# The second attention product as four 64x64 matmuls per tile, and a new order of work in a fused attention and routed-MLP kernel

## The chip, the core and the metric

The kernel runs on one core of a Trainium2 chip. The metric is the device time of one execution in microseconds. Each engine (TensorE, VectorE, ScalarE, GpSimd, and SyncE, which only starts transfers) has its own list of instructions and takes them in the order in which they were written; an instruction that waits holds up all that is behind it on its engine.

## The reference

Two stages follow each other. The first is an attention without scores between positions: for each of 8 batches and 8 heads, with 576 positions of 64 numbers,

```
q_s = softmax(q, over the 64 numbers)      # exp, divided by its sum
k_s = softmax(k, over the 576 positions)
kv  = k_s^T v                              # 64x64 for each head
x   = q_s kv                               # 576x64, heads side by side: 576x512
```

The second picks, in each batch, the 128 positions with the largest `x . w_gate`, and adds `sigmoid(score) * relu(xe w1) w2` to these rows alone (w1 is 512x1024, w2 1024x512). All data are float32.

## The kernel before, in words

A unit is a batch and four of its heads: 16 units, two to a batch. Positions lie on partitions so that a unit's q, k and v are tiles of 128 partitions, 4 heads, R = 5 rows, 64 numbers. Three buffers for each of q, k, v hold the units to come. A main loop has 20 slots `s`. In slot s the kernel ends unit s and begins unit s+1, and from slot 4 on it also does half of a batch's MLP: `mlp1` in even slots, `mlp2` in odd ones, each in 8 pieces that the program strews between the attention's steps. The names of the steps:

- `k_exp`, `q_exp`: the exponentials, on ScalarE. `v_copy`: copies v beside a column of ones, on VectorE.
- `kv_mm` (line 233): 20 matmuls with 128 rows and 64 columns of weights; two of them fill the width of the array. `kv_out` takes the sums out of PSUM and makes the operand of the next product, with one more column for the gate score.
- `q_t`, `q_t_last` (lines 260, 269): the transposes of exp(q); ScalarE (line 262) and VectorE (line 271) copy them to SBUF as `qT`, scaled by 1/sum of k.
- `x_mm(s, i)` (line 280): the second product for two heads, i = 0 and 1. Before, the two heads' 64x64 kv stand on the diagonal of a 128x128 operand `kv_diag` whose other half is zero, and 5 full matmuls of 132 columns do it.
- `x_out` (lines 292 to 298): VectorE divides by the sum of exp(q), writes `xs`, and keeps the score column. `x_store` sends `xs` to memory from SyncE's queue, behind which the loads of unit s+4 stand.
- `score`, `score_row`, `compare`, `pick`, `gate`: once per batch, the ranks of the scores. `score_row` (line 331) turns the scores by TensorE, five `compare` (line 344) count ranks on VectorE, `pick` (lines 364, 368) finds the rows by a VectorE operation `hit` and five small matmuls, and gathers them.
- `turn` (line 397), `mlp1` (411), `mlp2` (421), `finish` (429): the MLP of a picked batch.

Each float32 matmul stands in the trace as two records with their own weight loads: 5 matmuls of `x_mm` are 10 records, 20 of `kv_mm` are 40. The order inside the loop is written out by hand (`tc.manual_schedule`); before, the setup ahead of it is ordered by a scheduler.

Of the kernel before, what the change touches and what calls it, by code (L numbers as in the profile page):

```python
# [17 lines left out]
def kernel(  # L18
# [20 lines left out]
    nc = tc.nc  # L39
# [12 lines left out]
    G = 12  # L52
# [5 lines left out]
    WARM = 12  # L58
# [30 lines left out]
    def load(u, which, queues=(nc.sync, nc.sync)):  # L89
        b, qd = units[u]  # L90
        for what in which:
# [3 lines left out]
            for n, rows in enumerate((R, N2)):  # L95
                queues[n].dma_start(  # L96
                    out=t[n::2, :, :rows].rearrange("p h r d -> p h (r d)"),
                    in_=bass.AP(tensor=src.tensor, offset=first + n * R * D,
                                ap=[[9 * D, 64], [SD, 4], [1, rows * D]]))

    for n in range(LD):
        for what in "kvq":
            (nc.vector if n == 0 else nc.gpsimd).memset(raw[what][n][:, :, N2], 0.0)
    load(0, "k", (nc.sync, nc.scalar))
    load(0, "vq")
# [7 lines left out]
    warm = const.tile([P, 1], F32, name="warm")  # L113
    nc.scalar.activation(out=warm, in_=ones_b[:, :1], func=AF.Exp)
    ones_f = const.tile([P, P + 4], F32, name="ones_f")
    nc.vector.memset(ones_f, 1.0)
    w_ps = bank("tp", 2)
    w_ps2 = bank("tp", 2)
    for n in range(24):
        a, c = ((0, 0), (1, 1), (0, 1), (1, 0))[n % 4 if n >= 12 else n % 2]  # L120
        nc.tensor.matmul(out=(w_ps, w_ps2)[a][part(c), :66], lhsT=ones_f[part(a), :64],
                         rhs=ones_f[part(a), :66], start=True, stop=True)
    for n in range(WARM):
        nc.tensor.matmul(out=w_ps[:, :P], lhsT=ones_b[:, :P], rhs=ones_b[:, :P], start=True, stop=True)

    wg = const.tile([P, NQ, 2, D], F32, name="wg")
    for h in range(2):
        nc.scalar.dma_start(out=wg[part(h)].rearrange("p a i d -> p (a i) d"),
                            in_=bass.AP(tensor=moe_w_gate.tensor, offset=moe_w_gate.offset + h * D,
                                        ap=[[0, 64], [2 * D, 2 * NQ], [1, D]]))  # L130
    w1 = const.tile([P, KD, F], F32, name="w1")
# [4 lines left out]

    side = const.tile([P, 2], F32, name="side")
    nc.vector.memset(side, 0.0)
# [8 lines left out]
    v_ones, kv_diag = [], []  # L147
    for n in range(2):
# [4 lines left out]
        t = const.tile([P, 2, 2, C], F32, name=f"kv_diag{n}")  # L153
        nc.vector.memset(t, 0.0)
        kv_diag.append(t)
    for h in range(2):
        nc.vector.memset(side[part(h), h:h + 1], 1.0)
    qrec = const.tile([P, NU, 2, G], F32, name="qrec")
    krec = const.tile([P, NU, 2], F32, name="krec")


    x_buf = []
    for n in range(2):
        t = ps.tile([P, 2, 512], F32, tag=f"x{n}", name=f"x{n}", bufs=1)
        nc.vector.memset(t[:, 1, 4 * C:6 * C], 1.0)
        x_buf.append(t)
# [22 lines left out]
    def late_constants():  # L189

        nc.vector.tensor_single_scalar(odd_p, odd_p, 1, op=OP.bitwise_and)
        nc.vector.tensor_tensor(out=whole, in0=whole, in1=odd_p.to_broadcast([P, B * R]), op=OP.add)
        nc.vector.tensor_single_scalar(whole, whole, 1, op=OP.arith_shift_right)
        nc.vector.tensor_single_scalar(rest, whole, 31, op=OP.bitwise_and)
        nc.vector.tensor_tensor(out=whole, in0=whole, in1=rest, op=OP.subtract)
        nc.vector.tensor_copy(out=vals[:, :, :, 0], in_=whole.rearrange("p (b r) -> p b r", b=B))
        nc.vector.tensor_copy(out=vals[:, :, :, 1], in_=rest.rearrange("p (b r) -> p b r", b=B))
        nc.vector.memset(valid_r[:, 0], 1.0)
        nc.vector.memset(valid_r[:, 1], 0.0)
        nc.vector.memset(valid_r[:, 2], UP)  # L200
        nc.vector.tensor_copy(out=valid_r[:, 0, N2:], in_=valid)
        nc.vector.tensor_copy(out=valid_r[:, 1, N2:], in_=beyond)
        nc.vector.tensor_scalar(valid_r[:, 2, N2:], valid, UP, None, op0=OP.mult)
        for r in range(R):
# [324 lines left out]
    with tc.manual_schedule():  # L529
# [11 lines left out]
        for s in range(NU + LAG):  # L541
# [19 lines left out]
            if s == NU:  # L561
                chosen = B - 1
# [92 lines left out]
```

## Time and profile before

| | us |
|---|---|
| median of 3 runs (276.93 to 279.32) | 279.23 |
| the profiled execution | 278.86 |
| its span in the trace | 277.0 |
| TensorE matmul busy | 226.2 (82%) |
| VectorE busy | 131.1 (47%) |
| ScalarE busy | 92.0 (33%) |
| GpSimd busy | 27.8 (10%) |

Busy time is a sum over the whole span; the span has a start (to 14.7 us), four slots without MLP work (to 68.9), twelve with it (to 229), and an end in which only the last batches' MLP is left. A slot begins here with the first transpose of `q_t`. The granted clock of TensorE has two levels, shown as 1.00 (2.4 GHz) and 0.50 (1.2 GHz); a stretch that holds both shows a value between.

### The profile page before, as it was taken

The page shows a single profiled execution, that of the slowest core. Times are in us where ns is not written, and L with a number is a line of the kernel's source. Part 1 is how long each engine was busy: PE and PEld are TensorE (multiplying, and loading weights), DVE is VectorE, ACT ScalarE, POOL GpSimd, SP SyncE. Part 2 cuts the span into 40 slices and gives each one's busy share as a digit, 9 for nine tenths or more (in the row PEclk, how much of TensorE's full clock was granted, in tenths as well). Part 3 has the DMA queues.
Part 4 walks back from the last instruction along what each step waited for, and adds up shares of the span by engine and source line. Part 5 has one row for each costly group of instructions (what it writes and reads, how often), then busy time and mean ns, then how long its engine had stood idle before and what let it go on. Part 6 is the DMA issues. An engine that isn't in the chain of part 4 may idle for free.

```text
span 277.0 us, 4988 instructions
## 1 busy us (share of the span) xinstructions
PE 226.2 (82%) x1933; PEld 181.1 (65%) x1933; DVE 131.1 (47%) x435; ACT 92.0 (33%) x162; POOL 27.8 (10%) x74
## 2 busy tenths in 40 slices
PE   5367656566998999899989998999889998598990
PEld 4356646455895679567956795679567974584940
DVE  3275433943375347634764476447644656521001
ACT  2254422603434343434343434343435321110000
POOL 4000010011001110111011101110111011200001
PEclk9999775757899999999999999999999999799997
DMA  5999999296919292929292919291302032010101
GB/s 166 351 346 322 317 359 315 91 297 213 278 34 300 98 286 73 305 93 283 75 311 85 296 65 290 107 289 69 116 28 102 3 119 93 38 38 2 40 7 41
DMA packets 39328, 46.68 MB, mean 169 GB/s; under 512 B 2944, under 2 KB 36736, under 8 KB 39296
## 3 DMA queue, kind: packets, MB, share of 16 engines
q1 hardware_dynamic: 37200, 41.69, 47.2%
q0 software_dynamic: 1280, 4.20, 4.2%
q10 hardware_dynamic: 816, 0.39, 0.6%
q8 instruction: 17, 0.28, 0.4%
q14 instruction: 15, 0.12, 0.1%
HBM read 34.73 MB, written 11.53 MB: 167 GB/s over the span
## 4 chain that ended last, share of the span: by engine, by line
PE 56%; DVE 21%; DMA 9%; issue 5%; ACT 4%; SPq 3%; POOL 0%; POOLq 0%; ACTq 0%; DVEq 0%
PE mm L411 14%; PE mm L421 12%; PE x L280 12%; PE tp L233 9%; DMA v<-in_v_dram 7%; DVE xs L295 6%; PE tp L260 5%; DVE junk L344 4%; DVE v_ones L223 4%; SPq L96 2%; DMA q<-in_q_dram 2%; DVE qrec L292 2%; PE tp L331 2%; ACT qT L262 2%; SPq L303 1%
## 5 line engine op out<-in xcount | busy, mean ns | idle before, releaser
L411 PE MATMUL mm<-xT,w 128*128 128x128 f32 x512 | 62.8, 281 | 0.7 <-ACT xT L399 0.7
L421 PE MATMUL mm<-w,hT 128*128 128x512 f32 x128 | 62.1, 601 | 0.0
L411 PEld LDWEIGHTS mm<-xT,w 128*128 128x128 f32 x512 | 60.4, 196 | 1.4 <-ACT xT L399 1.0
L280 PEld LDWEIGHTS x<-kv_diag,qT 128*128 128x128 f32 x320 | 45.5, 216 | 6.2 <-issue 5.7
L280 PE MATMUL x<-kv_diag,qT 128*128 128x132 f32 x320 | 48.1, 304 | 0.0
L233 PE MATMUL tp<-v_ones,ke 128*64 128x65 f32 x640 | 26.0, 244 | 21.9 <-DVE v_ones L223 17.3
L233 PEld LDWEIGHTS tp<-v_ones,ke 128*64 128x64 f32 x640 | 24.1, 157 | 28.1 <-issue 28.1
L344 DVE SCALAR_TENSOR_TENSOR junk<-srow,s,not_before 128x576 bf16<-128x576 f32 x40 | 32.6, 816 | 2.4 <-ACT srow L336 1.5
L245 ACT COPY kv_diag<-tp 64x130 f32<-64x130 f32 x32 | 8.4, 262 | 66.8 <-DVE krec L242 66.4
L421 PEld LDWEIGHTS mm<-w,hT 128*128 128x128 f32 x128 | 21.4, 190 | 13.3 <-issue 12.9
L262 ACT ACTIVATE qT<-tp,krec 128x512 f32<-128x512 f32 x32 | 22.0, 687 | 22.7 <-PE tp L260 21.1
L295 DVE TENSOR_TENSOR xs<-x,qrec 128x384 f32<-128x384 f32 x64 | 28.5, 486 | 1.1
L260 PE MATMUL tp<-ident,qe 128*128 128x128 f32 x128 | 23.0, 309 | 5.7 <-ACT qT L262 2.7
L260 PEld LDWEIGHTS tp<-ident,qe 128*128 128x128 f32 x128 | 16.5, 158 | 15.5 <-ACT qT L262 8.9
L292 DVE RECIPROCAL qrec<-x 128x12 f32<-128x12 f32 x32 | 7.4, 232 | 35.1 <-PE x L280 33.4
L429 DVE SCALAR_TENSOR_TENSOR o<-mm,g,xr 128x512 f32<-128x512 f32 x8 | 6.0, 751 | 34.3 <-PE mm L421 34.3
L219 ACT ACTIVATE qe<-q 128x640 f32<-128x640 f32 x32 | 21.7, 725 | 0.2
L212 ACT ACTIVATE ke<-k 128x1280 f32<-128x1280 f32 x16 | 20.2, 1261 | 3.8 <-DMA k<-in_k_dram 3.8
L414 ACT ACTIVATE hT<-mm 128x512 f32<-128x512 f32 x16 | 9.6, 597 | 35.6 <-PE mm L411 35.6
L376 POOL DMA_INDIRECT xr<-out_dram,idx x8 | 7.9, 992 | 112.7 <-DVE no L374 109.9
L242 DVE RECIPROCAL krec<-tp 128x2 f32<-128x2 f32 x16 | 2.7, 171 | 28.4 <-PE tp L233 28.4
L223 DVE COPY v_ones<-v 128x1280 f32<-128x1280 f32 x16 | 13.1, 818 | 6.2 <-DMA v<-in_v_dram 6.2
(89 smaller groups left out, 131.5 us busy)
## 6 DMA issues: line engine op xcount, KB each, us to landing
k<-in_k_dram SPq DMA_DIRECT2D x16, 320.0 KB, 5.9
v<-in_v_dram SPq DMA_DIRECT2D x16, 320.0 KB, 7.1
q<-in_q_dram SPq DMA_DIRECT2D x16, 320.0 KB, 5.6
out_dram<-xs SPq DMA_DIRECT2D x16, 320.0 KB, 2.8
v<-in_v_dram SPq DMA_DIRECT2D x16, 256.0 KB, 6.1
q<-in_q_dram SPq DMA_DIRECT2D x16, 256.0 KB, 5.9
out_dram<-xs SPq DMA_DIRECT2D x16, 256.0 KB, 2.9
k<-in_k_dram SPq DMA_DIRECT2D x15, 256.0 KB, 7.4
```

The source lines that it names most:

```text
L212: nc.scalar.activation(out=ke, in_=raw["k"][u % LD], func=AF.Exp)
L219: nc.scalar.activation(out=qe[:, i], in_=qr[:, i], func=AF.Exp)
L223: nc.vector.tensor_copy(out=v_ones[u % 2][:, :, :, :D], in_=raw["v"][u % LD])
L233: nc.tensor.matmul(out=kv[part(h), i], lhsT=ke[:, 2 * i + h, r], rhs=vo[:, 2 * i + h, r], start=(r == 0), stop=(r == N2))
L260: nc.tensor.transpose(out=t_ps[:, r * P:(r + 1) * P], in_=qe[:, i, r].rearrange("p h d -> p (h d)"), identity=ident)
L262: nc.scalar.activation(out=st["qT", u][:, i, :N2].rearrange("p r c -> p (r c)"), in_=t_ps, func=AF.Copy, scale=krec[:, u, i:i + 1])
L280: nc.tensor.matmul(out=x[:, r // 3, g:g + 2], lhsT=qT[:, i, r], rhs=kv_diag[u % 2][:, i], start=True, stop=True)
L292: nc.vector.reciprocal(out=rec, in_=x[:, :, :, D])
L295: nc.vector.tensor_mul(xs[b][:, rows, qd, i], x[:, n, :g, :D].rearrange("p (r h) d -> p r h d", h=2), rec[:, n, :g].rearrange("p (r h) -> ...
L344: nc.vector.scalar_tensor_tensor(junk, st["srow", b], st["s", b][:, r:r + 1], not_before[:, r], op0=OP.subtract, op1=OP.is_ge, accum_out=s ...
L411: nc.tensor.matmul(out=h_ps[:, f % 4 * m:(f % 4 + 1) * m], lhsT=w1[:, d, f * P:(f + 1) * P], rhs=xT[:, d, :m], start=(d == 0), stop=(d == ...
L421: nc.tensor.matmul(out=st["y", b, n][:m], lhsT=st["hT", b, n][:, f, :m], rhs=w2[:, f], start=(f == 0), stop=(f == KF - 1))
```

## The change

`x_mm` uses the array as four 64x64 quarters: for each of the 5 rows, four matmuls of 66 columns with 64 rows and 64 columns of weights, so 20 instead of 5. Head h writes to its own PSUM bank. The operand `kv_w` has no zero half, so `kv_out` makes it by one copy instead of two, and the score column by the reduction itself. `x_out` takes all 5 rows in one multiplication instead of two.

The order changes too. The setup is under the manual order; v of unit 0 is loaded from ScalarE's queue; the warm-up is 24 matmuls of 128x512 instead of 24 small and 12 of 128. In all slots the first half of `q_exp(s+1)` stands ahead of `kv_out(s+1)`, `x_mm(s, 1)` ahead of `kv_mm(s+1)`, and `score_row` is in the next slot. From slot 4 on `v_copy(s+1)` stands ahead of `pick` and `x_out`, and all five `compare` behind `kv_out`. In slots 0 to 3 (`EARLY`) 6, 6 and 8 matmuls without use (`fill`) are put in, and in slot 2 the compares stand ahead of `v_copy`.

```diff
     def x_mm(u, i):
         qT = st["qT", u] if i == 0 else st.pop(("qT", u))
-        x = x_buf[i][:, :, :6 * C].rearrange("p n (g c) -> p n g c", g=6)
+        x = ps.tile([P, 2, 512], F32, tag="x", name="x", bufs=2)
         for r in range(R):
-            g = r % 3 * 2
-            nc.tensor.matmul(out=x[:, r // 3, g:g + 2], lhsT=qT[:, i, r], rhs=kv_diag[u % 2][:, i],
-                             start=True, stop=True)
+            for h, c in ((0, 0), (1, 1), (0, 1), (1, 0)):
+                nc.tensor.matmul(out=x[part(c), h, r * C:(r + 1) * C], lhsT=qT[part(h), i, r, part(c)],
+                                 rhs=kv_w[u % 2][part(h), i], start=True, stop=True)
+    def fill(n):
+        junk_ps = bank("mm", 2)
+        for _ in range(n):
+            nc.tensor.matmul(out=junk_ps[:, :P], lhsT=ones_b[:, :P], rhs=ones_b[:, :P], start=True, stop=True)
+
+    def kv_and_exp(u):
+        kv_mm(u)
+        q_exp(u, 0)
+        kv_out(u)
+        q_exp(u, 1)
...
+        if early:
+            fill(6)
+        if compared is not None and early:
+            score_row(compared)
+        if after and not early:
+            v_copy(s + 1)
+        pieces(1)
+        if chosen is not None:
+            pick(chosen)
+        if here:
+            x_mm(s, 0)
+            x_out(s, 0)
+        if compared is not None and not early:
+            score_row(compared)
+        if after:
+            k_exp(s + 1)
+        if compared is not None and early:
+            for r in range(R):
+                compare(compared, r)
+        if after and early:
+            v_copy(s + 1)
+        pieces(1)
+        if here:
+            x_mm(s, 1)
+            x_out(s, 1)
+            x_store(s)
+        if early:
+            fill(6)
+        if last:
+            score(ends)
+        pieces(1)
+        if after:
+            kv_and_exp(s + 1)
+        if early:
+            fill(8)
...
+        if compared is not None and not early:
+            for r in range(R):
+                compare(compared, r)
```

VectorE in an odd slot of the middle, from the scaling of the last transposes (`qT`) to the sums of the next unit (`krec`). Before:

```order
L271 TENSOR_TENSOR qT<-tp,krec 128x2x128
L364 TENSOR_TENSOR hit<-slot_no,rank 128x640
...
L292 RECIPROCAL qrec<-x_189 128x12
L295 TENSOR_TENSOR xs<-x_189,qrec 128x3x128
L295 TENSOR_TENSOR xs<-x_189,qrec 128x2x128
L298 TENSOR_TENSOR sr<-x_189,qrec 128x12
L223 COPY v_ones_175<-v_82 128x20x64
L242 RECIPROCAL krec<-tp 128x2
```

And with the change:

```order
L318 SCALAR_TENSOR_TENSOR junk,rank<-srow,s,not_before 128x576 x5
L246 TENSOR_TENSOR qT<-tp,krec 128x2x128
L202 COPY v_ones_160<-v_82 128x20x64
L338 TENSOR_TENSOR hit<-slot_no,rank 128x640
...
L269 RECIPROCAL qrec<-x 128x10
L270 TENSOR_TENSOR xs<-x,qrec 128x2x5x64
L272 TENSOR_TENSOR sr<-x,qrec 128x10
```

The copy of v moved from behind the division of x to ahead of `hit`, and five compares now stand directly ahead of the scaling of `qT`.

TensorE in an even slot of the middle, from the transposes to the end of the slot. Before:

```order
L397 MATMUL mm<-ident,xr 128x128 x4
L260 MATMUL tp<-ident,qe 128x128 x4
L280 MATMUL x_189<-kv_diag_178,qT 128x132 x5
L411 MATMUL mm<-xT,w_159 128x128 x8
L233 MATMUL tp<-v_ones_180,ke 64x65 x20
L411 MATMUL mm<-xT,w_159 128x128 x4
L280 MATMUL x_191<-kv_diag_178,qT 128x132 x5
L411 MATMUL mm<-xT,w_159 128x128 x20
```

And with the change:

```order
L371 MATMUL mm<-ident,xr 128x128 x4
L235 MATMUL tp<-ident,qe 128x128 x4
L385 MATMUL mm<-xT,w_146 128x128 x4
L256 MATMUL x<-kv_w_163,qT 64x66 x20
L305 MATMUL tp<-ident,s 128x128 x5
L385 MATMUL mm<-xT,w_146 128x128 x4
L256 MATMUL x<-kv_w_163,qT 64x66 x20
L385 MATMUL mm<-xT,w_146 128x128 x4
L212 MATMUL tp<-v_ones_164,ke 64x65 x20
L385 MATMUL mm<-xT,w_146 128x128 x20
```

Both halves of the second product now stand ahead of the next unit's first product, each in 20 matmuls instead of 5, and the five transposes of the scores come in here from the slot before.

ScalarE in the first slots, from the exponential of k to the next one. Before:

```order
L212 ACTIVATE ke<-k_80 128x1280
L245 COPY kv_diag_183<-tp 64x2x65 x2
L219 ACTIVATE qe<-q_77 128x640 x2
L262 ACTIVATE qT<-tp,krec 128x512 x2
L212 ACTIVATE ke<-k_81 128x1280
```

And with the change:

```order
L192 ACTIVATE ke<-k_80 128x1280
L199 ACTIVATE qe<-q_77 128x640
L223 COPY kv_w_167<-tp 128x2x65
L199 ACTIVATE qe<-q_77 128x640
L237 ACTIVATE qT<-tp,krec 128x512 x2
L192 ACTIVATE ke<-k_81 128x1280
```

Half of q's exponential moved ahead of the copy that waits for the first product, and that copy is one instruction.

## Rows read from the trace of the kernel before

**Rows 1.** The page, section 2: the span in 40 slices of 6.9 us.
```profile
PEclk9999775757899999999999999999999999799997
```

**Rows 2.** Stretches: length, busy us (instructions) of each engine, granted clock, DMA share, GB/s.
```profile
14.73:25.06 10.33, 7.54 (x70) 6.60 (x71) 6.40 (x29) 4.37 (x8) 0.00 (x0) 1.00 1.02 325
25.06:38.07 13.01, 7.76 (x75) 6.79 (x76) 6.04 (x22) 5.63 (x10) 0.98 (x5) 0.86 0.99 342
38.07:50.22 12.15, 9.59 (x71) 8.79 (x72) 3.88 (x11) 4.48 (x8) 0.00 (x0) 0.50 0.84 282
50.22:68.91 18.69, 10.12 (x81) 8.79 (x81) 10.60 (x37) 5.15 (x10) 2.15 (x6) 0.68 0.66 214
97.88:125.71 27.83, 25.62 (x236) 20.25 (x234) 15.22 (x48) 11.22 (x20) 3.00 (x7) 1.00 0.60 190
```

**Rows 3.** Waits of TensorE, 68.91 to 222.47 us: total, times, longest.
```profile
PE tp L233 <- DVE v_ones L223: 8.7, 11, 1.3
PE tp L331 <- DVE s L316: 1.8, 5, 0.4
```

**Rows 4.** Timeline of TensorE in an even middle slot: start, length, records [idle before].
```profile
131.08 1.39 PE L233 MATMUL tp<-v_ones,ke 128*64 128x65 f32 x40 [0.37 <-DVE v_ones L223]
132.40 1.16 PE L411 MATMUL mm<-xT,w 128*128 128x128 f32 x8
133.40 1.29 PE L280 MATMUL x<-kv_diag,qT 128*128 128x132 f32 x10
134.52 4.63 PE L411 MATMUL mm<-xT,w 128*128 128x128 f32 x40
```

**Rows 5.** Timeline of slot 1, all engines, the chain from one first product to the next.
```profile
24.27 1.36 ACT L219 ACTIVATE qe<-q 128x640 f32<-128x640 f32 x2
25.75 0.69 ACT L262 ACTIVATE qT<-tp,krec 128x512 f32<-128x512 f32 x1
26.99 1.29 PE L280 MATMUL x<-kv_diag,qT 128*128 128x132 f32 x10
28.32 0.23 DVE L292 RECIPROCAL qrec<-x 128x12 f32<-128x12 f32 x1 [1.75 <-PE x L280]
28.59 0.89 DVE L295 TENSOR_TENSOR xs<-x,qrec 128x384 f32<-128x384 f32 x2
29.47 0.82 DVE L223 COPY v_ones<-v 128x1280 f32<-128x1280 f32 x1
30.43 2.08 PE L233 MATMUL tp<-v_ones,ke 128*64 128x65 f32 x40 [2.15 <-DVE v_ones L223]
```

**Rows 6.** Timeline of TensorE at the start: the first product and the first transposes.
```profile
10.64 2.43 PE L233 MATMUL tp<-v_ones,ke 128*64 128x65 f32 x40 [4.58 <-DVE p_int L142]
14.73 1.09 PE L260 MATMUL tp<-ident,qe 128*128 128x128 f32 x4 [1.65 <-issue]
```

**Rows 7.** Timelines of TensorE: end of the warm-up; the small matmuls of a pick.
```profile
3.87 0.80 PE L121 MATMUL tp<-ones_f 64*64 64x66 f32 x17
...
4.60 1.46 PE L124 MATMUL tp<-ones_b 128*128 128x128 bf16 x12
...
141.06 0.28 PE L368 MATMUL tp<-vals,hit 128*128 128x5 bf16 x5
141.20 1.10 PE L421 MATMUL mm<-w,hT 128*128 128x512 f32 x2
```

**Rows 8.** Groups by line: busy us, mean ns.
```profile
L344 DVE SCALAR_TENSOR_TENSOR junk<-srow,s,not_before 128x576 bf16<-128x576 f32 x40 | 32.6, 816 | 2.4 <-ACT srow L336 1.5
L245 ACT COPY kv_diag<-tp 64x130 f32<-64x130 f32 x32 | 8.4, 262 | 66.8 <-DVE krec L242 66.4
L271 DVE TENSOR_TENSOR qT<-tp,krec 128x256 f32<-128x256 f32 x16 | 6.7, 420 | 8.9 <-PE tp L269 8.9
L364 DVE TENSOR_TENSOR hit<-slot_no,rank 128x640 bf16<-128x640 f32 x8 | 6.5, 815 | 0.0
```

**Rows 9.** Timeline of TensorE at the end: the last pick.
```profile
238.33 0.28 PE L368 MATMUL tp<-vals,hit 128*128 128x5 bf16 x5 [2.79 <-DVE hit L364]
```

More of the change, by code (lines that the diff above doesn't have):

```diff
@@ L87, with load @@
     raw = {w: [const.tile([P, 4, R, D], F32, name=f"{w}{n}") for n in range(LD)] for w in "qkv"}
[L89 removed]
+    def load(u, which, queue=nc.sync):
         b, qd = units[u]
@@ L94, in load @@
             first = src[b, 4 * qd].offset
-            for n, rows in enumerate((R, N2)):
-                queues[n].dma_start(
+            for n, rows in ((1, N2), (0, R)):
+                queue.dma_start(
                     out=t[n::2, :, :rows].rearrange("p h r d -> p h (r d)"),
@@ L112 @@
     nc.vector.memset(ones_b, 1.0)
[L113 to L116, printed above, removed]
     w_ps = bank("tp", 2)
[L118 to L122, printed above, removed]
     for n in range(WARM):
-        nc.tensor.matmul(out=w_ps[:, :P], lhsT=ones_b[:, :P], rhs=ones_b[:, :P], start=True, stop=True)
+        nc.tensor.matmul(out=w_ps, lhsT=ones_b[:, :P], rhs=ones_b, start=True, stop=True)
     wg = const.tile([P, NQ, 2, D], F32, name="wg")
@@ L130 @@
                                         ap=[[0, 64], [2 * D, 2 * NQ], [1, D]]))
+    warm = const.tile([P, 1], F32, name="warm")
+    nc.scalar.activation(out=warm, in_=ones_b[:, :1], func=AF.Exp)
     w1 = const.tile([P, KD, F], F32, name="w1")
@@ new lines, with pieces @@
+    EARLY = 4
+    def fill(n):
[4 more added lines that the diff above has]
+        kv_mm(u)
+        q_exp(u, 0)
+        kv_out(u)
+        q_exp(u, 1)
+    k_exp(0)
+    v_copy(0)
+    kv_and_exp(0)
+    load(3, "kvq")
+    load_w1(0)
+    load_w1(1)
+    number = None
+    for s in range(NU + LAG):
+        mlp_b, odd = divmod(s - LAG, 2)
+        busy = s >= LAG
+        first = busy and odd == 0
+        piece = mlp1 if first else mlp2
+        f_next = 0
+        def pieces(n):
+            nonlocal f_next
+            for _ in range(min(n, 8 - f_next) if busy else 0):
+                each(piece, mlp_b, f_next)
+                f_next += 1
+        here = s < NU
+        after = s + 1 < NU
+        last = s == NU - 1
+        early = s < EARLY
+        ends = s // 2 if here and s % 2 == 1 else None
+        compared = s // 2 - 1 if s % 2 == 0 and 2 <= s < NU else None
+        chosen = (s - 3) // 2 if s % 2 == 1 and 3 <= s < NU else None
+        if s == NU:
+            chosen = B - 1
+        if here:
+            q_t(s, 0)
+            q_t_last(s)
+        if first:
+            each(turn, mlp_b)
+        else:
+            pieces(1)
+        if here:
+            q_t(s, 1)
+        if early:
[7 more added lines that the diff above has]
+            pick(chosen)
+        if here:
+            x_mm(s, 0)
[10 more added lines that the diff above has]
+        pieces(1)
+        if here:
+            x_mm(s, 1)
[10 more added lines that the diff above has]
+            fill(8)
+        if s == 0:
+            load_w1(2)
+            load_w1(3)
+        if s + 4 < NU:
+            load(s + 4, "kvq")
+        if s in (1, 2):
+            load_w2(s - 1)
+        if compared is not None and not early:
+            for r in range(R):
+                compare(compared, r)
+        if last:
+            score_row(ends)
+            for r in range(R):
+                compare(ends, r)
+        if chosen is not None:
+            each(gate, chosen)
+        if ends is not None and not last:
+            score(ends)
+        pieces(8)
+        if busy and odd == 1:
+            each(finish, mlp_b)
+        if s == NU:
+            number = sums_in_range()
```

184 lines of the change are left out of this document (36 added, 148 removed).

## The prediction, made before the changed kernel was run

> **What bounds the kernel now.** I read the page's line of the granted clock first, then stretches slot by slot, then the waits of TensorE, and last the timelines where a wait stood. The clock is not at its full level everywhere: the slices from about 30 to 70 us show 5 to 9, all later ones but the last pick's show full [rows 1]. Slots 0 to 3 take 10.33, 13.01, 12.15 and 18.69 us, with TensorE busy 7.5 to 10.1 us of them [rows 2]. A pair of middle slots takes 27.83 us with TensorE busy 25.62 [rows 2]. So there are two regimes. In the middle TensorE is the bound and what can be won is its own work and its few waits. At the start the bound is a chain that goes through all engines, one unit behind the other, and it runs partly at the low level of the clock.
>
> In the middle the waits are few and named: between 68.91 and 222.47 us, 8.7 us for the copy of v and 1.8 us for the scores [rows 3]. The copy of v is late because it stands behind the division of x on VectorE, not because v is late.
>
> At the start the chain can be followed in slot 1 [rows 5]: exp(q), the copy of the transposes, the x product, the division, the copy of v, the next first product. TensorE waits 2.15 us for the copy of v there. The transfers are no far-off second: their share is 1.02 and 0.99 in slots 0 and 1 [rows 2].
>
> **The x product at full clock.** Before, a stage of 10 records takes 1.12 us from its start to that of the next matmuls (133.40 to 134.52 [rows 4]). Now it has 40 records. No row shows 64x64 quarters at the full level, so I bound a record's price. The warm-up ran the same shape in four quarters: the last 17 records took 0.80 us; less one record's own 0.31, 16 steps are 0.030 us each [rows 7]. I take this to be at the low level, since the first product behind it takes 2.43 us instead of 1.39 [rows 4, 6]. If clock alone sets it, a record costs 0.015 at full level: 0.6 us a stage, plus 0.07 to leave. If something else limits how closely records follow each other, the nearest rows at full level speak: the first product has 40 records in 1.32 us (131.08 to 132.40 [rows 4]), which is 39 steps of 0.030 and 0.15 to the next full matmul; five matmuls of 5 columns take 0.14 us, 0.028 each [rows 7]. I take 0.029, nearest to two rows at the right level: 40 x 0.029 = 1.16, and 0.12 more to leave the quarters, as the first product shows, 1.27 us. That is 0.15 us more than now, over 24 stages of the twelve middle slots **+3.6 us**. Ends: 0.67 us a stage (-10.8 us) and 1.48 us (40 x 0.030, 0.12, and 0.16 to enter, since a record of 10 in 1.29 us runs 0.28 with a step of 0.11: +8.6 us). The Trainium skill (TensorE: Matmul & The Clock Gate, the section on 56 ns) gives about 25 ns as the least from one matmul's start to the next, however small; by it a stage would be 1.12 us and this term nil, which no row here at this shape shows.
>
> **Waits in the middle.** The copy of v now stands ahead of `hit` and of the division, so the 8.7 us go; the score's transposes stand a slot later, so the 1.8 us go [rows 3]. What is late next is `hit` in the odd slots: ahead of it VectorE now has five compares of 0.82 us, the scaling of 0.42, the copy of 0.82 and `hit` itself, 0.82 [rows 5, 8], which with some 1.3 us of the first product's evacuation make 7.5 to 7.7 us. TensorE gets there after five pieces of 8 records at 0.112 (4.5 us), ten transposes at 0.11 and two pieces of 0.86: 7.3 us. I count 0.4 us, between 0 and 0.8 (one VectorE operation more), six times: +2.4. **Sum -8.1 us.** ScalarE's order also changes, but exp(k) still has the x product and two MLP pieces ahead of the first product that needs it, about 1 us more than it takes; if that cover went, its excess would be paid in each slot. The single copy and the single multiplication save VectorE and ScalarE some tenths a slot, off the path in the middle.
>
> **The start.** The first product ran from 10.64 to 13.07, the transposes came 1.65 us later [rows 6]. Now k and v are started from two queues, and the 24 matmuls of 512 columns must end first. 128 columns took 0.105 us (12 in 1.46, less one's own 0.31 [rows 7]), so 24 x 0.42 = 10 us at the low level, 5 at the full one: starting at 2.3, they end between 9.5 (the clock rises on the way) and 12.6. I take 9.9, and the full level for the first product, 1.35: it ends at 11.25 (bounds 10.9 and 15.0).
>
> Then a slot's chain, from the end of one first product to the end of the next. Of the 1.65 us, half of exp(q) (0.68 [rows 5]) is now done ahead and one copy of 0.26 [rows 8] goes: 0.7. Then the second half 0.68, copy of transposes 0.69, transposes and restart 0.55 (26.44 to 26.99), six `fill` at 0.052: 2.95 in all. From the x product's start to the next first product's start is 3.44 (26.99 to 30.43 [rows 5]), now +0.15, and 1.32 to its end. **7.9 us a slot** at full clock. Ends: 19.2 for slot 0, 27.1 for slot 1. Slot 2 has the score's transposes (0.6) and five compares ahead of the copy of v (4.3), so TensorE has a hole of more than 4 us; before, a hole of 2.15 us came just ahead of the fall of the clock [rows 1, 5]. I count the next first product at the low level (+1.04 [rows 4, 6]): 40.9. Slot 3 has `hit` ahead of x (0.5) and some low clock (1.5): 50.8. Slot 4 then starts at 51.3 instead of 68.91: **-17.6 us**. Transfers: five units of 1.77 MB, w1 (2.1 MB) and one store (0.6) are 11.5 MB, which at 325 to 342 GB/s [rows 2] from about 3 us on are there at 38; slot 3 wants unit 4 at 43. If compute were faster than this, the loads would stop it.
>
> **The end.** One MLP piece (0.9 us) moves ahead of the last pick into its 2.79 us of idle time [rows 9]: **-0.9**. The clock dips at that place [rows 1]; should it no longer do so, the matmuls behind it would be shorter too, which I don't count.
>
> **Sum.** The profiled execution took 278.86 us: 278.86 - 17.6 - 8.1 + 3.6 - 0.9 = 255.9. It lies 0.4 under the median of the runs, so I forecast **256 us**, with its own range of 251 to 261.
>
> **Rivals.**
> 1. *The quarters are cheap.* The price falls with the clock to 0.015 to 0.02 us a record. For it: the warm-up's four quarters did overlap fully [rows 7]. Against it: no row at full clock is under 0.028. Time: 256 - 3.6 - 10.8 = 242 at the end, 242 to 250. Chance 0.25.
> 2. *The start is held.* The fills don't hold the clock, or the loads come late. At the low level each of four slots pays 1.04 for the first product and about 0.5 for transposes and fills: 6 us, 262 (257 to 266). For it: DMA shares of 1.0, and a clock that fell in slot 1, with TensorE busy 7.76 of 13.01 us [rows 2]. Chance 0.17.
> 3. *Entering costs as much as leaving.* Each stage waits until full matmuls have run out, 0.16 us x 24 = 3.8: 260. The rows show leaving (0.12), not entering. The Trainium skill (TensorEngine Tiling (Array Packing), Key Properties) says that changing the tiling mode drains TensorE, and this speaks against the change; by that rule it is paid at both ends, and the exit in the trace agrees with it. Chance 0.08.
> 4. *Slower.* At full clock the quarters don't overlap: a record then costs the 0.055 us that 66 of its columns take alone (half of 132's 0.112), a stage 2.3 us, +1.2 x 24 = 29, and some 5 at the start: 278.9 - 26.6 + 34 = 286. It turns the sign from 2.2 us a stage on (26.6/24 + 1.12). Against it: the first product's 0.033 for two parts and the warm-up's 0.030 [rows 4, 7]. Chance 0.02.
> 5. *It doesn't do what it says.* The waits move to `hit` and exp(k) whole, and compute at the start waits for loads: within 1% of now. Chance 0.03.
>
> My forecast has 0.45. Two measurements of this kernel can't be told apart within about 1%. So faster by over 1% has 0.95, within 1% 0.03, slower 0.02. The range that leaves out no more than 2 in 10 reaches into rivals 1 to 3: 244 to 263.
>
> **What would show it.** The x stages: 40 records in 1.16 us, 1.27 to the next matmul; 0.67 would be rival 1, 2.3 rival 4. TensorE's waits for the copy of v from slot 4 on gone, and a new one of 0.4 for `hit` in odd slots. A pair of middle slots of 27.83 - 2.0 + 0.4 + 0.6 = 26.8 us. Slot 4 starting near 51 us, with one dip of the clock in slots 2 and 3. The forecast fails if slot 4 starts later than 58 us or a pair is under 25.5 or over 27.5 us.

## The result, and the profile after

| | before | after |
|---|---|---|
| median, us | 278.08 (276.45 to 279.32) | 239.25 (238.54 to 240.16) |
| profiled execution, us | 278.86 | 240.16 |
| its span, us | 277.0 | 238.4 |
| TensorE matmul busy, us | 226.2 | 211.9 |

The changed kernel takes 0.8608 of the time of the kernel before, 95% interval 0.8544 to 0.8673. The forecast was 256 us, in a range of 244 to 263: the direction was right, the gain larger than the range allowed. Two measures are used below: medians for the comparison of kernels, and spans of profiled executions for where the time went.

The stretches of the changed kernel, with the columns of [rows 2]: slots 0 to 3, then an even and an odd slot of the middle.

```profile
11.39:18.41 7.02, 5.61 (x150) 4.81 (x151) 4.05 (x11) 4.08 (x7) 0.00 (x0) 1.00 1.08 357
18.41:26.60 8.19, 5.92 (x154) 4.94 (x151) 4.06 (x11) 3.96 (x7) 0.00 (x0) 1.00 1.06 365
26.60:40.03 13.43, 7.85 (x159) 6.65 (x156) 8.69 (x25) 5.09 (x10) 0.98 (x5) 0.76 1.07 383
40.03:47.96 7.93, 6.14 (x157) 5.40 (x156) 4.95 (x15) 3.69 (x6) 1.17 (x1) 0.98 1.06 372
98.71:111.78 13.07, 12.89 (x204) 12.00 (x203) 8.02 (x20) 5.84 (x10) 1.71 (x1) 1.00 0.80 259
111.78:123.25 11.47, 11.47 (x154) 6.52 (x152) 6.86 (x22) 4.65 (x8) 1.95 (x6) 1.00 0.64 201
```

Slot 4 starts at 47.96 instead of 68.91. The odd slot is TensorE work from end to end: 11.47 busy of 11.47. A pair of middle slots, 98.71 to 123.25 here, takes 24.54 us, and 24.53 in the next pair, against 27.83 before.

The granted clock, to be laid beside [rows 1] (40 slices of 6.0 us):

```profile
PEclk9999986999999999999999999999999998899997
```

One dip is left near 36 us, and one behind the last pick. Now the waits of TensorE between the starts of slots 4 and 15, 47.96 to 185.39 us, to be laid beside [rows 3]:

```profile
PE mm L371 <- DMA xr<-out_dram,idx: 1.1, 1, 1.1
PE tp L235 <- ACT qT L237: 0.9, 5, 0.2
PE mm L385 <- ACT xT L373: 0.2, 1, 0.2
```

No wait for the copy of v, none for the scores, and none for `hit` is left there. The timeline of TensorE in an even and an odd slot shows what the x product costs now, to be laid beside [rows 4]:

```profile
100.65 1.16 PE L385 MATMUL mm<-xT,w 128*128 128x128 f32 x8
101.73 0.81 PE L256 MATMUL x<-kv_w,qT 64*64 64x66 f32 x40
102.48 0.76 PE L305 MATMUL tp<-ident,s 128*128 128x128 f32 x5
...
113.73 1.02 PE L395 MATMUL mm<-w,hT 128*128 128x512 f32 x2
114.59 0.27 PE L342 MATMUL tp<-vals,hit 128*128 128x5 bf16 x5
114.80 0.81 PE L256 MATMUL x<-kv_w,qT 64*64 64x66 f32 x40
115.54 1.13 PE L395 MATMUL mm<-w,hT 128*128 128x512 f32 x2
116.60 0.81 PE L256 MATMUL x<-kv_w,qT 64*64 64x66 f32 x40
```

A stage of 40 records takes 0.75 us from its start to that of the next matmul (101.73 to 102.48; 0.74 from 114.80). One record alone takes 0.22 (the page of the profile: 1280 in all, mean 223 ns), so 39 steps share 0.81 - 0.22 = 0.59 us: 0.015 us each. Going into the quarters and out of them costs time too, and that shows in the full matmuls on either side. Eight MLP records ahead of a stage take 1.08 us to its start (100.65 to 101.73); the same eight take 1.00 in the run with the order alone, where a full product follows (its rows are shown there). So the way in costs about 0.08. Two records of 512 columns between two stages, with a way out and a way in, take 1.06 (115.54 to 116.60) against 0.86 for such a pair that runs free (113.73 to 114.59): 0.20 more for both. A stage with both is then about 0.93 us, against 1.12 before.

By part of the program, the spans differ as follows. The forecast of slots 4 to 14 is made of -8.7 and -1.8 for the waits, five waits of 0.4 for `hit`, and 22 stages at +0.15; the sixth wait, two stages and the -0.9 of the end belong to the last row.

| | before | after | difference | forecast |
|---|---|---|---|---|
| start, to slot 4 | 68.91 | 47.96 | -20.95 | -17.6 |
| slots 4 to 14 | 153.56 | 137.43 | -16.13 | -5.2 |
| slot 15 and the end | 54.53 | 53.01 | -1.52 | -0.2 |

Most of the error, 10.9 of some 15.6 us, is in the middle.

### The profile page after: what moved, and what is told of

It is laid out like the page before. It is cut to its first block, busy times and chain, and to the rows that moved or that the text cites. A ratio compares the mean times of both kernels' runs of the same rounds, so it can differ in the third digit from the quotient of the medians.

```text
span 238.4 us, 6902 instructions
## 1 busy us (share of the span) xinstructions
PE 211.9 (89%) x2937; PEld 159.4 (67%) x2937; DVE 126.7 (53%) x379; ACT 85.9 (36%) x146; POOL 30.8 (13%) x74
## 3 DMA queue, kind: packets, MB, share of 16 engines
q0 software_dynamic: 1280, 4.20, 5.2%
## 4 chain that ended last, share of the span: by engine, by line
PE 73%; DMA 11%; DVE 5%; ACT 5%; issue 2%; POOL 1%; SPq 0%; POOLq 0%; ACTq 0%
PE mm L385 26%; PE mm L395 23%; DMA q<-in_q_dram 8%; PE x L256 8%; PE tp L212 7%; PE tp L235 5%; DMA xr<-out_dram,idx 3%; ACT qT L237 2%; PE tp L305 2%; DVE junk L318 2%; ACT qe L199 1%; DVE o L403 1%; DVE v_ones L202 1%; PE tp L244 1%; ACT xT L373 0%
## 5 line engine op out<-in xcount | busy, mean ns | idle before, releaser
L385 PE MATMUL mm<-xT,w 128*128 128x128 f32 x512 | 65.3, 284 | 1.6 <-ACT xT L373 1.6
L212 PE MATMUL tp<-v_ones,ke 128*64 128x65 f32 x640 | 23.5, 229 | 9.5 <-DVE qrec L269 8.6
L212 PEld LDWEIGHTS tp<-v_ones,ke 128*64 128x64 f32 x640 | 21.2, 143 | 15.1 <-issue 12.0
L270 DVE TENSOR_TENSOR xs<-x,qrec 128x640 f32<-128x640 f32 x32 | 26.4, 824 | 1.1
L256 PEld LDWEIGHTS x<-kv_w,qT 64*64 64x64 f32 x1280 | 21.5, 133 | 6.7 <-ACT qe L199 3.8
L256 PE MATMUL x<-kv_w,qT 64*64 64x66 f32 x1280 | 25.6, 223 | 0.0
L269 DVE RECIPROCAL qrec<-x 128x10 f32<-128x10 f32 x32 | 7.0, 220 | 31.7 <-PE x L256 31.7
L235 PE MATMUL tp<-ident,qe 128*128 128x128 f32 x128 | 19.9, 279 | 2.9 <-ACT qT L237 2.4
L223 ACT COPY kv_w<-tp 128x130 f32<-128x130 f32 x16 | 4.3, 266 | 45.3 <-DVE krec L221 45.3
L404 POOL DMA_INDIRECT out_dram<-o,idx x8 | 11.2, 1397 | 40.4 <-DVE o L403 40.4
```

What stands on the lines that cost most here:

```text
L212: nc.tensor.matmul(out=kv[part(h), i], lhsT=ke[:, 2 * i + h, r], rhs=vo[:, 2 * i + h, r], start=(r == 0), stop=(r == N2))
L235: nc.tensor.transpose(out=t_ps[:, r * P:(r + 1) * P], in_=qe[:, i, r].rearrange("p h d -> p (h d)"), identity=ident)
L256: nc.tensor.matmul(out=x[part(c), h, r * C:(r + 1) * C], lhsT=qT[part(h), i, r, part(c)], rhs=kv_w[u % 2][part(h), i], start=True, stop=True)
L270: nc.vector.tensor_mul(xs[b][:, :, qd, i].rearrange("p r h d -> p h r d"), x[:, :, :, :D], rec.to_broadcast([P, 2, R, D]))
L385: nc.tensor.matmul(out=h_ps[:, f % 4 * m:(f % 4 + 1) * m], lhsT=w1[:, d, f * P:(f + 1) * P], rhs=xT[:, d, :m], start=(d == 0), stop=(d == ...
L404: nc.gpsimd.indirect_dma_start(out=out_rows[:(b + 1) * S], out_offset=bass.IndirectOffsetOnAxis(ap=idx[:m, :1], axis=0), in_=o[:m], in_off ...
```

## The experiments

The theory from here on: in the middle the quarters are cheap, 0.015 us a record, and the new order removes the waits; the start is shortened by the order. The rivals differ by experiment and stand in the expectations.

**The order without the quarters.** The order of the changed kernel, with the product by 5 full matmuls, its diagonal operand made by two copies, and the division in two multiplications. Of the edit, the product:

```
-        x = ps.tile([P, 2, 512], F32, tag="x", name="x", bufs=2)
+        x = x_buf[i][:, :, :6 * C].rearrange("p n (g c) -> p n g c", g=6)
         for r in range(R):
-            for h, c in ((0, 0), (1, 1), (0, 1), (1, 0)):
-                nc.tensor.matmul(out=x[part(c), h, r * C:(r + 1) * C], lhsT=qT[part(h), i, r, part(c)],
-                                 rhs=kv_w[u % 2][part(h), i], start=True, stop=True)
-        st["x", u] = x
+            g = r % 3 * 2
+            nc.tensor.matmul(out=x[:, r // 3, g:g + 2], lhsT=qT[:, i, r], rhs=kv_diag[u % 2][:, i],
+                             start=True, stop=True)
```

> The changed kernel with the product of before: full matmuls on the diagonal operand, two copies in kv_out, two multiplications in x_out; the new order and setup stay. Theory 1 (a quarter record costs 0.015 us at full clock, a stage 0.74 and 0.19 more to enter): each of 24 stages beside MLP work becomes 1.12 without entry, +0.19, together +4.6; in slots 0 to 3 the chain loses about 0.9 a slot (first x stage 0.45, two copies 0.36, division 0.1), +3.6: about 247 us. Rival (a stage is worth 1.27 all in, as I forecast): this one is the faster, about 235. Rival (the product is off the path, the order does it all): 239.

Measured: 248.4 us (248.31 to 249.28), ratio 0.894 (0.887 to 0.900). The order alone is worth about 30 us, the quarters on top of it 9. The wait for `hit` that the forecast put at 6 x 0.4 us is seen in this kernel, at half its size. TensorE over the whole span (total, times, longest):

```profile
PE tp L359 <- DVE hit L355: 2.0, 6, 0.9
```

The 0.9 is the last pick; the five others are 0.2 each. The first stage of an even slot, with the matmuls ahead of it:

```profile
104.81 1.16 PE L402 MATMUL mm<-xT,w 128*128 128x128 f32 x8
105.81 1.29 PE L271 MATMUL x<-kv_diag,qT 128*128 128x132 f32 x10
```

Slot 4 starts at 49.53 in this kernel and slot 15 at 193.81, so slots 4 to 14 take 144.28 us.

**The quarters without the order.** The kernel before, with the product, its operand and the division of the changed one (the diff above turned round, on the kernel before).

> The kernel before with the product of the change alone (quarters, one copy, one multiplication), in the old order. Theory 1: 24 stages at -0.19 are -4.6, the four first slots lose about 1 us each since their low clock makes a full stage 2.2 and quarters 1.2: -4; the waits for the copy of v stay: about 269 us. Rival (what the product gives, the copy of v takes back): 276 to 278. With the run of the order alone this shows whether the two parts add up to the 39 us.

Measured: 270.4 us (269.35 to 270.99), ratio 0.973 (0.965 to 0.980). The two parts alone give -30.5 and -8.6 us in their own comparisons, together -39.1, and the whole change gives -38.8: the totals add up within the noise of some 3 us, and neither part needs the other to gain. By part of the program they are not the same gain, though. In the old order the quarters take 4.3 us from the start and 4.4 from slots 4 to 14 (slot 4 starts at 64.57 here, slot 15 at 213.76); on top of the new order they take 1.6 and 6.9. In slots 4 to 14 of this kernel TensorE idles as long as before (11.55 us after 11.39), so the 4.4 are the product alone: 0.20 for each of the 22 stages. TensorE's longest wait over this kernel's whole span:

```profile
PE tp L219 <- DVE v_ones L209: 18.5, 9, 2.8
```

Before, the copy of v cost 17.3 us over the whole span: with the old order the cheaper product does not shorten this wait.

**Two quarters at a time.** The same 20 matmuls a stage, in an order in which only two different quarters follow each other.

```
-        for r in range(R):
-            for h, c in ((0, 0), (1, 1), (0, 1), (1, 0)):
+        for two in (((0, 0), (1, 1)), ((0, 1), (1, 0))):
+            for r, (h, c) in [(r, hc) for r in range(R) for hc in two]:
```

> The changed kernel with the 20 quarter matmuls of a stage in another order: the two on the diagonal for all five rows, then the two others, so that only two quarters can run side by side. Same instructions, same results. By the spacing measured apart (two quarters 0.030 us a record, four 0.015) a stage costs 0.6 us more, which is the 0.029 of my forecast: 24 stages beside MLP work +14 us, in slots 0 to 3 one stage a slot on the chain +2.4: about 256. Rival (the matmuls of a stage overlap whatever their order, or the stage is not on the path): 239 to 241.

Measured: 248.8 us (247.87 to 249.3), ratio 0.8945. The mechanism is right and the size was too large. The timeline of TensorE in an even slot of this kernel:

```profile
106.14 1.21 PE L256 MATMUL x<-kv_w,qT 64*64 64x66 f32 x40
107.28 0.76 PE L305 MATMUL tp<-ident,s 128*128 128x128 f32 x5
```

A stage takes 1.14 us, 0.40 more than with four quarters in turn; 24 such stages are 9.6 us, and the medians differ by 9.5. So the gain of the product comes from four quarters working side by side. In this kernel the step is (1.21 - 0.22)/39 = 0.0255, and not the 0.030 of the next experiment from which 256 was worked out. Why the two differ stays open.

**The price of a record, by itself.** Behind the warm-up, at the full clock (granted 1.00 from 11.54 to 30.81 us), stages of small matmuls on constants between full ones; the rest of the kernel is the changed one and starts later for it, so the total time says nothing.

```
+    full(12, 128)
+    quarters(20, 66, four)
+    full(8, 128)
+    quarters(20, 34, four)
+    full(8, 128)
+    quarters(20, 18, four)
+    full(8, 128)
+    quarters(20, 66, four[:2])
+    full(8, 128)
+    quarters(10, 66, four[:1])
+    full(8, 128)
+    halves(20, 65)
+    full(8, 128)
+    halves(20, 18)
+    full(8, 128)
+    full(20, 18)
+    full(8, 128)
```

`quarters` uses 64x64 of weights in four, two or one quarter of the array in turn; `halves` has 128 rows and 64 columns of weights in two halves, as the first product; the last number of each is the moving columns.

> Measures the disputed price: after the warm-up, at full clock, groups of float32 matmuls on ones, with 8 full ones between: four quarters at 66, 34 and 18 columns, two quarters and one quarter at 66, two halves (128 rows, 64 columns) at 65 and 18, full at 18. Step between records. Theory 1 (columns over clock over tiles in parallel, a small fixed part, no limit near 0.028): four quarters 0.015, 0.008 to 0.010, 0.006 to 0.010; two 0.028; one 0.055; halves 0.029 at 65 and about 0.010 at 18. Rival (records can't follow each other closer than about 0.025 unless something in the x stage differs): all groups level off at 0.025 to 0.029. Entering quarters after full ones: 0.19, leaving 0.13. The kernel as a whole is longer by some 15 us; that is not its point.

The timeline of TensorE:

```profile
11.54 0.81 PE L131 MATMUL mm<-ones_f 64*64 64x66 f32 x40
12.29 2.05 PE L126 MATMUL tp<-ones_f 128*128 128x128 f32 x16
14.27 0.79 PE L131 MATMUL mm<-ones_f 64*64 64x34 f32 x40
...
16.96 0.77 PE L131 MATMUL mm<-ones_f 64*64 64x18 f32 x40
...
19.65 1.38 PE L131 MATMUL mm<-ones_f 64*64 64x66 f32 x40
...
22.95 1.38 PE L131 MATMUL mm<-ones_f 64*64 64x66 f32 x20
...
26.23 1.39 PE L136 MATMUL mm<-ones_f 128*64 128x65 f32 x40
...
29.53 1.35 PE L136 MATMUL mm<-ones_f 128*64 128x18 f32 x40
```

The rows differ in two ways. By the number of tiles in turn, with 66 columns: four give 40 records in 0.81 us, two give 40 in 1.38, one gives 20 in 1.38; less one record's own 0.22 that is 0.015, 0.030 and 0.061 us a step. The step halves with each doubling of the tiles. By moving columns: 66, 34 and 18 take 0.81, 0.79 and 0.77, and 65 against 18 in the halves 1.39 against 1.35. So neither theory of the price held whole: records in tiles side by side follow each other closer than 0.025 to 0.029, and the step does not shrink with the columns either, as the theory of cheap quarters had it. A tile with 64 columns of weights takes about 0.06 us a record, whatever moves through it (between 18 and 66), divided by the tiles that work side by side. That it is the loading of the weights which sets these 0.06 us fits all seven rows but isn't shown apart from them.

The full matmuls between give the price of going in and out: 16 records take 1.98 us from one group to the next (12.29 to 14.27), where 16 free-running ones of 0.112 take 1.79. That is 0.19 for a way out and a way in, as in the changed kernel, and it is the same beside the halves (27.55 to 29.53).

**The copy of v in its old place.** From slot 4 on the copy of v behind the division of x again; the rest as changed.

```
-        if after and not early:
-            v_copy(s + 1)
...
-        if after and early:
+        if after:
             v_copy(s + 1)
```

> The changed kernel, but from slot 4 on the copy of v stands behind the first division again, as before. Theory: the copy's own place is not what removed its wait; with the second x stage moved ahead of the next first product, TensorE has a stage (0.93) and two MLP pieces (1.8) in hand against 2.1 us of division and copy: 239 to 240 us, no wait for the copy. Rival (the copy's place removed the 8.7 us, as I wrote): about 248, with waits of 0.4 and 1.3 back.

Measured: 240.6 us (239.45 to 241.12), ratio 0.865: no difference from the changed kernel. In the middle the waits for the copy do not come back: the four kinds of wait that are left there have 2.0 us in all, and one of 0.5 in slot 5, right behind the copy, is the only one of them that may be its. Behind slot 5 a pair takes 24.53 us, as in the changed kernel. So the wait of 8.7 us did not go because the copy moved past `pick` and the division. What is left of the new order to explain it is the second x stage: with both halves of the x product, and the MLP pieces between them, ahead of the next unit's first product, the copy has time in either place. That stage was not moved back by itself.

**Without the fills.** The three groups of `fill` in slots 0 to 3 are left out.

```
-        if early:
-            fill(6)
...
-        if early:
-            fill(6)
...
-        if early:
-            fill(8)
```

> The changed kernel without the 80 matmuls of no use in slots 0 to 3. Theory (they hold the clock): TensorE then idles for more of each slot and the clock falls in slot 0 or 1; slots 0 to 3 pay the low level in first product, transposes and x stage, 1.0 + 0.4 + 0.5 a slot in two or three of the four, less 0.3 for six fills on the chain: +3 to +5, 243 to 244. Rival (the holes are too short to let the clock fall, fills cost their own time): 4 x 0.3 less, 238.

Measured: 237.1 us (236.25 to 237.57), ratio 0.8536. The theory that the fills hold the clock fell. The timeline of TensorE in slots 0 to 2:

```profile
11.33 0.63 PE L235 MATMUL tp<-ident,qe 128*128 128x128 f32 x4 [0.55 <-issue]
...
17.56 0.66 PE L235 MATMUL tp<-ident,qe 128*128 128x128 f32 x4
...
22.91 1.39 PE L212 MATMUL tp<-v_ones,ke 128*64 128x65 f32 x40 [1.25 <-DVE qrec L269]
24.23 0.65 PE L235 MATMUL tp<-ident,qe 128*128 128x128 f32 x4
...
34.87 2.44 PE L212 MATMUL tp<-v_ones,ke 128*64 128x65 f32 x40 [5.71 <-DVE qrec L269]
```

The first product takes 1.39 us in slot 1, so the clock is at its full level without them, and slots 0 and 1 take 6.23 and 6.67 us, against 7.02 and 8.19 with them (0.95 of the 8.19 is a gap in which TensorE waited for nothing that the profile shows). In slot 2 the clock falls behind a hole of 5.71 us, as it does with the fills. In these slots they only lengthen the chain.

**The compares behind the copy.** In slot 2 the copy of v ahead of the five compares. (In the expectation, the hole is the one in slot 2.)

```
+        if after and early:
+            v_copy(s + 1)
         if compared is not None and early:
             for r in range(R):
                 compare(compared, r)
-        if after and early:
-            v_copy(s + 1)
```

> The changed kernel with slot 2's five compares behind the copy of v instead of ahead of it. Theory: the hole of 5.27 us in front of slot 2's first product shrinks to about 1, the compares then delay the second division and kv_out, so the chain gains 4.3 of copy time less what VectorE still owes, 1.5 to 2.5 us, and the clock may stay up: 236.5 to 238. Rival (the loads bound the first slots, their DMA share is 1.07): slot 3 or 4 waits for a load instead, 239.

Measured: 237.7 us (236.78 to 238.55), ratio 0.8556. TensorE in slot 2 of this kernel:

```profile
32.36 1.52 PE L212 MATMUL tp<-v_ones,ke 128*64 128x65 f32 x40 [1.08 <-DVE v_ones L202]
...
38.22 0.64 PE L244 MATMUL tp<-ident,qe 128*128 128x128 f32 x2 [3.34 <-DVE prod L225]
```

The hole of 5.27 went down to 1.08, and 3.34 of it came back one step later, at the transposes that need what VectorE makes from the first product: it is still at the compares then. The hole that VectorE's work makes here moved with that work.

**Both at the start.** No fills, and the compares of slot 2 behind the evacuation of the first product, as in the later slots.

```
-        if compared is not None and early:
-            for r in range(R):
-                compare(compared, r)
...
-        if compared is not None and not early:
+        if compared is not None:
             for r in range(R):
                 compare(compared, r)
```

> The changed kernel without the fills, and with slot 2's compares behind the next first product's evacuation, as in the later slots. The fills alone gave 2.2 us and the compares behind the copy of v 1.5. Theory (the first four slots are one chain, and each was a piece of it): the two add up, 235 to 236 us; slot 3 then waits for the scaling of the last transposes behind the compares, some 3 us, in place of 5.3 in front of slot 2's first product. Rival (VectorE or the loads bound slots 2 and 3 together): no better than without the fills, 237.

Measured: 236.4 us (235.66 to 238.46), ratio 0.851 (0.846 to 0.856), which overlaps with leaving out the fills alone (237.1). The rival was right:

```profile
30.63 1.39 PE L212 MATMUL tp<-v_ones,ke 128*64 128x65 f32 x40 [1.52 <-DVE qrec L269]
...
38.49 0.29 PE L342 MATMUL tp<-vals,hit 128*128 128x5 bf16 x5 [4.03 <-DVE hit L338]
...
43.36 2.44 PE L212 MATMUL tp<-v_ones,ke 128*64 128x65 f32 x40 [1.36 <-DVE qrec L269]
```

The first product of slot 2 now runs at the full clock, and TensorE waits 4.03 us for `hit` in slot 3 instead; behind that wait the clock is low. In each of the three places that were tried for the compares, TensorE waits for VectorE in slot 2 or 3.

**The x stages together.** From slot 4 on both x stages stand directly ahead of the first product, so that the quarters are entered once a slot. Of the edit:

```
-        if here:
+        if here and early:
             x_mm(s, 0)
...
-        pieces(1)
+        pieces(2 if here and not early else 1)
+        if here and not early:
+            x_mm(s, 0)
+            x_mm(s, 1)
+            x_out(s, 0)
...
-        pieces(1)
+        if early or last or not here:
+            pieces(1)
```

> The changed kernel, from slot 4 on both x stages and the next first product directly one behind the other, the MLP pieces between them moved ahead. Theory (each change between full matmuls and quarters costs 0.19 to enter and 0.13 to leave): one entry and one exit fewer between the x stages, and the exit and entry between x and the first product at most shared: 0.3 to 0.6 in each of 11 slots, 3.5 to 6.5 us less: 233 to 236, unless the first product then waits for exp(k) or a PSUM bank. Rival (entering costs nothing, the 0.19 is MLP work spread out): 239.

Measured: 239.0 us (237.92 to 241.77), ratio 0.8572: a miss in the total. A pair of middle slots takes 23.85 us instead of 24.53, 0.34 a slot as priced, so the eleven slots did give 3.7. In the profiled execution slot 4 started at 50.47, 2.5 later than in the changed kernel's although the code up to there is the same, and the last pick waited 1.81 for `hit` instead of 0.95. These take back most of the 3.7 in that execution. But the median of all runs moved by under 1.5 us as well, and why the 3.7 are missing there isn't shown.

**Both edits together.** No fills, compares behind the evacuation, x stages together from slot 4 to 14.

> The same with both x stages and the next first product directly behind each other from slot 4 to 14, slot 15 as in the changed kernel. With the stages together a pair of slots took 23.85 us instead of 24.53, but the last pick came 0.86 later. Theory (0.32 of entry and exit saved in each of 11 slots, 3.5 us, given back elsewhere only in slot 15): 3 to 3.5 us under the same kernel without it, 231 to 233. Rival (what is won in the middle is lost to a later hit or load again): no difference.

Measured: 232.6 us (231.75 to 235.35), ratio 0.838 (0.832 to 0.843), the best version. Its span of 229.9 is 3.9 under that of the start's edits alone, about what eleven slots by 0.34 make (3.7). TensorE in an even slot of this kernel:

```profile
123.55 1.40 PE L256 MATMUL x<-kv_w,qT 64*64 64x66 f32 x80
124.87 1.39 PE L212 MATMUL tp<-v_ones,ke 128*64 128x65 f32 x40
```

80 records take 1.32 us here to the next first product, which is in tiles of 64 columns itself, and 1.44 in an odd slot (111.90 to 113.34).

**The changed kernel once more**, beside the other experiments.

> The changed kernel itself, on the same chip as the two others: 238.5 to 240.5 us. Its slot 4 started at 47.96 us in one execution, and at 50.1 and 50.5 in two kernels with the same first slots: a start of 48 to 51 again, and an end with or without a dip of the clock behind the last pick (1.6 us).

Measured: 239.8 us (238.25 to 240.49), ratio 0.8619 (0.8577 to 0.8662). Slot 4 starts at 48.33. The dip of the clock behind the last pick is not there:

```profile
200.11 0.28 PE L342 MATMUL tp<-vals,hit 128*128 128x5 bf16 x5 [0.95 <-DVE hit L338]
200.25 6.50 PE L385 MATMUL mm<-xT,w 128*128 128x128 f32 x56
```

In the first profile the same 56 records behind the same wait of 0.95 took 8.12 us:

```profile
200.56 8.12 PE L385 MATMUL mm<-xT,w 128*128 128x128 f32 x56
```

So 1.6 us at the end, and about 2 at the start, differ between executions of the same code, and differences of that size between two profiles are not put down to an edit here.

## Why the prediction was too cautious, step by step

**The price of a quarter record: the step that failed.** The prediction took 0.029 us a record at the full clock, "nearest to two rows at the right level", and so +3.6 us for the product; it was 0.015. The two rows were the first product, two tiles at a time, and full matmuls of 5 columns [rows 4, 7]. They were read as a limit on how closely records follow each other. For the first row the experiment shows that it is the price of its own tiles: two side by side give 0.030, four give 0.015. The second, matmuls of another type on the whole array, was not tried, but it set no limit here. The row with the right shape was the warm-up at the low level of the clock (0.030 [rows 7]), and scaling it by the clock, rival 1, gives what was measured. For 22 stages the prediction had 22 x 0.15 = +3.3 us, and the measured 0.93 against 1.12 is -4.2 (-4.4 in the run of the quarters alone): 7.5 us of the error of 10.9. The sentence on the Trainium skill (TensorE: Matmul & The Clock Gate, the section on 56 ns), that starts are never closer than about 25 ns, is not borne out by the records of four tiles in turn: 39 steps of 0.015 us. Counted by the kernel's matmuls, of two records each, a step is 0.030.

**Entering the quarters (rival 3).** The rival came true beside rival 1: beyond the 0.75 us from a stage's start to the next matmul, up to 0.20 are lost in the full matmuls on either side, about 0.08 on the way in and the rest on the way out. The prediction had a way out of 0.12 within the stage and had left the rest out as not shown. By the Trainium skill (TensorEngine Tiling (Array Packing), Key Properties) a change of mode drains TensorE; these 0.19 to 0.20, and the 0.34 a slot saved by entering once instead of twice, agree with it. Rival 1 without this would have given a stage of 0.75 and 4 us more.

**The waits of the middle.** The 8.7 and 1.8 us went, as forecast, but the reason given for the 8.7 was not the one that counts: the prediction had them go because the copy of v stands ahead of `hit` and of the division, and with the copy back behind the division they stay away just the same. That the number came true is luck in so far. The 0.4 us for `hit` in six odd slots did not come: 0 in the middle. VectorE from the first of the five compares to `hit`, in the changed kernel:

```profile
108.36 0.81 DVE L318 SCALAR_TENSOR_TENSOR junk<-srow,s,not_before 128x576 bf16<-128x576 f32 x1
...
112.64 0.42 DVE L246 TENSOR_TENSOR qT<-tp,krec 128x256 f32<-128x256 f32 x1
112.98 0.82 DVE L202 COPY v_ones<-v 128x1280 f32<-128x1280 f32 x1
113.71 0.82 DVE L338 TENSOR_TENSOR hit<-slot_no,rank 128x640 bf16<-128x640 f32 x1
```

From the start of the matmul behind the first product, 107.21, VectorE needs 7.32 us to the end of `hit` at 114.53, where 7.5 to 7.7 were counted, and TensorE gets to the pick at 114.59, 7.38 us behind it, where 7.3 were counted. The margin is 0.06 us; the forecast's 0.4 was a small difference of two sums of that size. Slots 4 to 14, before and after, with the columns of [rows 2]:

```profile
68.91:222.47 153.56, 142.17 (x1308) 114.77 (x1309) 84.14 (x263) 61.77 (x110) 15.02 (x35) 0.99 0.52 164
47.96:185.39 137.43, 135.14 (x1977) 104.67 (x1975) 83.11 (x236) 59.01 (x103) 19.08 (x40) 1.00 0.63 206
```

All the idle time of TensorE in them went from 153.56 - 142.17 = 11.39 us to 137.43 - 135.14 = 2.29: -9.1, where -8.5 was forecast.

**What was not counted.** The idle time gives -9.1 and the product -4.2, together -13.3 of -16.13. The rest, 2.8, may be the overlap that a wait costs beside its idle time. In the kernel before, the same four MLP records stand once ahead of a wait and once free of one:

```profile
121.15 1.88 PE L421 MATMUL mm<-w,hT 128*128 128x512 f32 x4
123.39 0.76 PE L331 MATMUL tp<-ident,s 128*128 128x128 f32 x5 [0.36 <-DVE s L316]
123.99 1.88 PE L421 MATMUL mm<-w,hT 128*128 128x512 f32 x4
```

They take 2.24 us to the next start with the wait of 0.36, and 1.72 without one (123.99 to 125.71): 0.16 more than the wait. For 16 such waits [rows 3] that is an estimated 2.6 us. The run of the order alone bears it out in part: with the same matmuls as before, these 16 waits gone and five for `hit` new, slots 4 to 14 get 9.3 us shorter and their idle time 8.1 (11.39 to 3.28). That is 1.2 beyond the idle time, where 0.16 for each of eleven waits would make 1.8.

**The start.** The mechanism held: the chain of [rows 5] got shorter, with one dip of the clock in slot 2. The order did most of it: without the quarters slot 4 starts at 49.53 already. Apart from the fills and the compares, the edits of the order at the start were not tried one by one. Slot 0 took 7.02 and slot 1 8.19 where 7.9 each was forecast. The hole in slot 2 came as forecast, and the first product behind it ran at the low level:

```profile
36.83 2.44 PE L212 MATMUL tp<-v_ones,ke 128*64 128x65 f32 x40 [5.27 <-DVE qrec L269]
```

Slot 3 took 7.93 where 9.9 was counted. Slot 4 began at 47.96 to 50.5 in profiles of kernels with this start, against a forecast of 51.3. One assumption was wrong without harm to the sum: the fills, for which 0.3 us a slot were paid, did nothing for the clock in slots 0 and 1: it is at its full level there without them too. Transfers did not stop the start, but they are close: their share is 1.06 to 1.08 in slots 0 to 3, and the chain of waits of the changed kernel goes from 30 to 50 us through them (the loads of q behind SyncE's queue, then the gather, for which TensorE waits 1.1 us in slot 4). That may be a second reason, beside VectorE, why the edits at the start brought 2 to 3 us and not the 5 of the hole; no run took the transfers apart.

**The end.** The last pick's idle time fell from 2.79 to 0.95 [rows 9]; forecast -0.9, measured -1.84 in that wait. Slot 15 and the end together gave -1.52.

**The rivals' chances.** Rival 1 had 0.25 and a time of 242 at its end, and 239.25 lies under it. With 3.4 less at the start and 2.4 less for `hit` it is 236; with the measured 0.93 a stage instead of its 0.67, for rival 3 has its part, 242 again; the 2.8 us that were not counted lead to 239. The prediction gave a time for each rival by itself and none for the two together. The forecast's own condition for failing, a pair under 25.5 us, was met.

## What to carry to other kernels

Price a small matmul by its own shape and by how many tiles work side by side, not by the nearest row of another shape: a row at the wrong clock but with the right shape was the better witness. Where tiles of the array are used, group the stages, since a way in and a way out cost time, here about 0.2 us together in the full matmuls beside them. A hole that one engine's queue makes can return at the next wait for that engine; at the start of this kernel two moves of the same five operations brought 3.34 and 4.03 us of it back elsewhere.

## What the runs showed of the hardware

The step between float32 records of 64x64 tiles was 0.015 us with four tiles in turn, 0.030 with two and 0.061 with one (66 moving columns); with four in turn it was nearly the same for 18, 34 and 66 moving columns.

The clock fell while TensorE was shown busy without a gap. In the experiment on the price, behind the halves, full matmuls of 18 columns run between others of 128; the stretches there, with the columns of [rows 2]:

```profile
34.00:35.00 1.00, 1.00 (x11) 1.00 (x11) 0.00 (x0) 0.00 (x0) 0.00 (x0) 1.00 0.00 0
35.00:36.00 1.00, 1.00 (x10) 1.00 (x10) 0.00 (x0) 0.00 (x0) 0.00 (x0) 0.84 0.00 0
36.00:42.00 6.00, 6.00 (x28) 5.85 (x28) 0.00 (x0) 0.00 (x0) 0.00 (x0) 0.50 0.01 3
```

TensorE is shown busy in all of this time, as in the microseconds ahead, and the granted clock goes from 1.00 to 0.50 (2.4 to 1.2 GHz) within the second row. What made it fall there was not tried.
